# Four more hidden units by seven products, half loads of `y0`, first values in rows, a new written order

## The chip, the cores and the metric

The kernel runs on one core of one Trainium2 chip. The metric is the device time of one execution in microseconds (us), as the median of several runs of the same program; lower is better.

## The reference

Three computations follow each other on 2304 tokens (4 batches of 576): an attention whose softmaxes stand on q and k apart, a gated layer (called layer a here), and a second layer with Softplus (layer b). Cut to what is computed:

```python
def _attn_ref(q, k, v):            # (4, 8, 576, 64)
    q_s = softmax of q over the 64 features
    k_s = softmax of k over the 576 positions
    kv = np.einsum('bhsd,bhse->bhde', k_s, v)
    return np.einsum('bhsd,bhde->bhse', q_s, kv)

def _moe_ref(x, w_gate, w_val, w_out, rms_g):   # 512 -> 1536 -> 512
    xn = x / np.sqrt(np.mean(x * x, axis=-1, keepdims=True) + 1e-06) * rms_g
    g = xn @ w_gate
    return g * (1.0 / (1.0 + np.exp(-g))) * (xn @ w_val) @ w_out

def _moe2_ref(x, w_in, w_out):                  # 512 -> 2048 -> 512
    h = x @ w_in
    g = np.maximum(h, 0.0) + np.log1p(np.exp(-np.abs(h)))
    return g @ w_out
```

The attention's result, put back to 2304 rows of 512, goes through `_moe_ref` and then `_moe2_ref`. q and k are drawn with factors of 8 and 5.126.

## The kernel before

**Arithmetic.** Nearly every product is made of halves: a number is split into a high part and what is left of it, and `mm3` (L932 to L935) issues three matmuls, high by high (L933), high by low (L934) and low by high (L935). Large products go "by seven": a product of 2 x 2 blocks is made from seven block products of sums and differences of the blocks instead of eight, as in Strassen's method, and its sums run on the other engines.

**Tiling.** Tokens come in blocks of 384 (`T`); two blocks make a run. In layer b there are three runs, and each goes through the hidden dimension in eight units of 256 (`NPB` = 8): units 0 to 7 belong to the first run, 8 to 15 to the second, 16 to 23 to the third. Per unit: seven `H` steps (`h_mul`, L1271) make the hidden values; `HC` and `HD` copy and add them, `SP` (L1297) is Softplus on ScalarE; `SU` (`act_sum`) makes sums of them for products by seven; `BH` and `BL` (`act_h`, `act_l`, L1237 to L1247) make the high and low halves. Then the unit's part of the output: by four block products, as `Y` steps (`y_mul`, L1304: 512 columns per matmul, added up over the units in six PSUM banks, one for each of two token halves `o` and three chunks `t` of 128 tokens, and copied out by `YE`), or by seven, as `YP` steps (`y_part`, L1353: 21 per unit, 256 columns per matmul; products 1 to 4 are taken out of PSUM for each unit by `YC` or `YA`, the latter an addition on VectorE at L1380, products 5 to 7 add up in PSUM; `YX` joins the results of a run). Which units go by seven is the set `BY7` (L1262): before, units 8 to 21. The first run's eight units go by `Y`.

**Weights.** Weights arrive as 64-bit floats; `F` fetches a part, `CA` (Abs on ScalarE, L491), `CL` and `CD` (VectorE or GpSimd, L496 to L510) turn it into 32-bit floats. `TU` and `PS` make sums of blocks, `WH` (L587) and `WL` (L593) halves, `KO` (`keep_w`, L595) stores them into DRAM (`kept<-ws`), `WB` (`load_b`, L1266) loads them for each unit that uses them (`w<-kept`). The units of the first run thus read weights that were stored not long before: their names are `hx1`, `hx2`, `hx3`, `hx4` (first layer's blocks) and `y0`, `y1`, `yc`, `yd` (second layer's). `yc` and `yd` are the sums by seven: `VA`, `VS`, `VH`, `VL` (L1419 to L1448) make them for later runs and `VK` stores them.

**The order.** All is written out by hand: `ORDER` (L25 to L325) is a list of 4005 steps, executed by the loop at L1488. A step is a name and indices; a last letter says the engine (V VectorE, A ScalarE, P GpSimd). Each engine's queue is served in the order in which the list issues to it, and all DMAs stand in one queue, SP's. `HOMES` (L327 to L353) says which buffer each taking of a pooled tile uses: 16 tiles `w` (1024 columns, a ring for weights), 3 `ws` (work tiles of weights), 8 PSUM banks, 6 `hl`, 7 `h`, 3 `bits`, 2 each of `raw`, `s`, `a`, `ln`. A step that takes a tile waits until the tile's last reader, often a DMA, is done.

**The start.** `LV` (`load_v`, L632) and `LW` (L639) load a batch's values into `v_t`, whose rows have 64 values of two heads and a column of ones; batch 0 takes eight DMAs, one for each head, in pieces of 256 bytes, and two for the rest. `K3` (L759) multiplies the exponentials of k by them; the column of ones gives the denominators. `B` steps (`busy`, L977) issue matmuls of the identity that nobody reads.

The lines that the change touches are `load_v`, `load_vx`, `k3`, `act_h`, `BY7`, `load_b`, `h_softplus`, `y_mul`, `act_sum`, `y_part`, `y_join`, `w2_h`, and the two lists.

## Time and profile before

| | |
|---|---|
| median of 3 runs | 906.39 us (904.86 to 910.32) |
| the profiled execution | 907.15 us |
| its span in the profile | 905.4 us |
| TensorE (PE) busy | 880.7 us, 97% |
| VectorE (DVE) busy | 739.7 us, 82% |
| ScalarE (ACT) busy | 445.4 us, 49% |
| GpSimd (POOL) busy | 337.4 us, 37% |
| moved by DMA | 226.70 MB, mean 250 GB/s |

The profile is of one execution, times in us from the start of its span. Busy time is that in which an engine executes; a wait is idle time with the event that ended it. Matmuls overlap, so the duration of one is longer than the distance to the next one's start. "SPq" is SyncE issuing DMAs. The granted clock (PEclk) is the share of full speed that the chip gives TensorE.

### The profile page before, as it was taken

The page shows a single profiled execution, that of the slowest core. Times are in us where ns is not written, and L with a number is a line of the kernel's source. Part 1 is how long each engine was busy: PE and PEld are TensorE (multiplying, and loading weights), DVE is VectorE, ACT ScalarE, POOL GpSimd, SP SyncE. Part 2 cuts the span into 40 slices and gives each one's busy share as a digit, 9 for nine tenths or more (in the row PEclk, how much of TensorE's full clock was granted, in tenths as well). Part 3 has the DMA queues.
Part 4 walks back from the last instruction along what each step waited for, and adds up shares of the span by engine and source line. Part 5 has one row for each costly group of instructions (what it writes and reads, how often), then busy time and mean ns, then how long its engine had stood idle before and what let it go on. Part 6 is the DMA issues. An engine that isn't in the chain of part 4 may idle for free.

```text
span 905.4 us, 14902 instructions
## 1 busy us (share of the span) xinstructions
PE 880.7 (97%) x5296; PEld 848.6 (94%) x5296; DVE 739.7 (82%) x1365; ACT 445.4 (49%) x885; POOL 337.4 (37%) x302
## 2 busy tenths in 40 slices
PE   8899999999999999999999999989899999999998
PEld 8799999999999999999999998778799999999996
DVE  7999788697789998998989985767688676887764
ACT  3686665233566645555557756455343233342221
POOL 4543453233533223212342334423445347343312
PEclk9999999999999999999999999989999999999999
DMA  9995342342878898887999998876989887796942
GB/s 254 222 247 134 98 127 84 94 128 70 278 287 330 316 318 302 299 284 285 323 345 336 319 325 286 299 274 220 326 317 326 287 285 242 254 307 216 347 154 70
DMA packets 118011, 226.70 MB, mean 250 GB/s; under 512 B 31024, under 2 KB 72240, under 8 KB 117936
## 3 DMA queue, kind: packets, MB, share of 16 engines
q1 hardware_dynamic: 117936, 225.74, 73.8%
q8 instruction: 42, 0.69, 0.3%
q14 instruction: 33, 0.27, 0.1%
HBM read 169.87 MB, written 55.84 MB: 249 GB/s over the span
## 4 chain that ended last, share of the span: by engine, by line
PE 73%; DVE 11%; DMA 8%; ACT 3%; issue 2%; SPq 1%; POOL 1%; ACTq 0%; DVEq 0%; POOLq 0%
PE ps L933 23%; PE ps L934 23%; PE ps L935 23%; DMA kept<-ws 3%; PE ps L861 2%; DMA w<-kept 2%; DMA spilled<-bits 2%; PE ps L766 1%; DVE bits L506 1%; DVE bits L510 1%; DMA raw<-in_moe_w_out_dram 1%; PE ps L888 1%; SPq L635 1%; DVE h L1247 1%; DVE bits L502 1%
## 5 line engine op out<-in xcount | busy, mean ns | idle before, releaser
L933 PE MATMUL ps<-hl,w 128*128 128x384 f32 x284 | 99.3, 350 | 0.0
L934 PE MATMUL ps<-hl,w 128*128 128x384 f32 x284 | 95.2, 335 | 1.2 <-DVE hl L930 1.2
L935 PE MATMUL ps<-hl,w 128*128 128x384 f32 x284 | 95.1, 335 | 0.0
L933 PE MATMUL ps<-xy,w 128*128 128x384 f32 x218 | 74.4, 341 | 3.1 <-DMA w<-kept 2.3
L935 PE MATMUL ps<-w,h 128*128 128x256 f32 (+1 forms) x215 | 70.8, 329 | 3.3 <-DVE h L1247 3.3
L934 PE MATMUL ps<-xy,w 128*128 128x384 f32 x218 | 73.5, 337 | 0.0
L935 PE MATMUL ps<-xy,w 128*128 128x384 f32 x218 | 73.5, 337 | 0.0
L933 PE MATMUL ps<-w,h 128*128 128x256 f32 (+1 forms) x215 | 70.4, 328 | 1.6 <-DMA w<-kept 1.1
L934 PE MATMUL ps<-w,h 128*128 128x256 f32 (+1 forms) x215 | 70.3, 327 | 0.0
L1380 DVE TENSOR_TENSOR x<-ps,x 128x512 f32<-128x512 f32 x72 | 49.0, 687 | 25.8 <-PE ps L935 25.5
L933 PE MATMUL ps<-h,w 128*128 128x384 f32 x192 | 64.5, 336 | 0.9 <-ACT ps L1251 0.9
L935 PE MATMUL ps<-h,w 128*128 128x384 f32 x192 | 64.2, 334 | 0.0
L934 PE MATMUL ps<-h,w 128*128 128x384 f32 x192 | 64.2, 334 | 0.0
L934 PEld LDWEIGHTS ps<-hl,w 128*128 128x128 f32 x284 | 53.4, 188 | 2.4 <-DVE hl L930 1.5
L933 PEld LDWEIGHTS ps<-hl,w 128*128 128x128 f32 x284 | 53.4, 188 | 2.0 <-ACT s L1004 0.4
L491 ACT ACTIVATE bits<-raw 128x512 f32<-128x512 f32 x53 | 35.4, 672 | 39.0 <-DMA spilled<-bits 10.7
L935 PEld LDWEIGHTS ps<-hl,w 128*128 128x128 f32 x284 | 53.3, 188 | 0.0
L1247 POOL TENSOR_TENSOR h<-a,h 128x384 fp32r<-128x384 f32 x24 | 27.0, 1127 | 63.6 <-DVE h L1243 39.4
L935 PEld LDWEIGHTS ps<-w,h 128*128 128x128 f32 x215 | 41.0, 191 | 7.2 <-DVE h L1247 3.7
L933 PEld LDWEIGHTS ps<-xy,w 128*128 128x128 f32 x218 | 41.2, 189 | 6.7 <-DVE ws L593 2.6
L933 PEld LDWEIGHTS ps<-w,h 128*128 128x128 f32 x215 | 41.1, 191 | 5.8 <-DMA w<-kept 1.1
L506 DVE SCALAR_TENSOR_TENSOR bits<-raw,bits 128x512 int32<-128x512 int32 x62 | 46.0, 743 | 0.6
(488 smaller groups left out, 2914.7 us busy)
## 6 DMA issues: line engine op xcount, KB each, us to landing
w<-kept SPq DMA_DIRECT2D x93, 512.0 KB, 5.6
kept<-ws SPq DMA_DIRECT2D x56, 512.0 KB, 5.6
xy<-outside SPq DMA_DIRECT2D x22, 768.0 KB, 7.9
raw<-in_moe_w_out_dram SPq DMA_DIRECT2D x26, 512.0 KB, 5.3
hl<-outside SPq DMA_DIRECT2D x24, 384.0 KB, 7.1
raw<-in_moe_w_in_dram SPq DMA_DIRECT2D x16, 512.0 KB, 5.1
outside<-hl SPq DMA_DIRECT2D x18, 384.0 KB, 3.7
qe<-outside SPq DMA_DIRECT2D x8, 768.0 KB, 7.3
```

The source lines that it names most:

```text
L491: nc.scalar.activation(out=b.bitcast(F32), in_=hi, func=AF.Abs)
L502: nc.vector.tensor_scalar(out=b, in0=b, scalar1=3, scalar2=0x3FFFFFF8, op0=ALU.logical_shift_left, op1=ALU.bitwise_and)
L506: nc.vector.scalar_tensor_tensor(out=b, in0=words[:, :, 1], scalar=-0x40000000, in1=b, op0=ALU.bitwise_and, op1=ALU.bitwise_or)
L510: nc.vector.scalar_tensor_tensor(out=b, in0=words[:, :, 0], scalar=29, in1=b, op0=ALU.logical_shift_right, op1=ALU.bitwise_or)
L635: nc.sync.dma_start(out=v_t[:, m, :R, o * D:(o + 1) * D], in_=v[b, h, :SM].rearrange("(p r) d -> p r d", r=R))
L766: nc.tensor.matmul(out=ps[:, i, :], lhsT=ke_t[lo][:, i, r], rhs=v_t[:, m, r, :], start=(r == 0), stop=(r == R))
L861: nc.tensor.matmul(out=ps[:, s:s + n], lhsT=kvb[b % 2][:, m, :], rhs=qT_t[:, m, s:s + n], start=True, stop=True)
L933: nc.tensor.matmul(out=ps, lhsT=wh, rhs=xh, start=first, stop=False, skip_group_check=more)
L934: nc.tensor.matmul(out=ps, lhsT=wh, rhs=xl, start=False, stop=False, skip_group_check=more)
L935: nc.tensor.matmul(out=ps, lhsT=wl, rhs=xh, start=False, stop=last, skip_group_check=more)
L1247: engine[e].tensor_tensor(out=h[:, 1], in0=part[u, (f, o)], in1=h[:, 0].bitcast(F32), op=ALU.subtract)
L1380: nc.vector.tensor_tensor(out=tot, in0=ybank.pop((u, pair, t)), in1=tot, op=ALU.add)
```

## The change

Four things are done at once.

1. Units 4 to 7 of the first run go by seven (`TURN` = 4; `BY7` now begins at 4). Its six sums of units 0 to 3 end at unit 3 (`last` in `y_mul`); the new step `YT` (`y_turn`, 12 steps) turns them, by one copy and three subtractions for each chunk, into the totals to which products 1 to 4 of units 4 to 7 are added; `y_join` gets a way of its own for run 0, in the totals' own tiles. `yc` and `yd` of units 4 to 7 are now wanted in the first run: `w2_h` makes them in a tile of the ring `w` instead of `ws`. Some activations of units 4 to 6 take `hl` tiles instead of `raw` and `bits` (`act_h`, `spare`).
2. Units 8 to 21 load only the first 256 columns of `y0` (512 KB become 256 KB), the half that products by seven read.
3. Batch 0's values are loaded in rows as they stand in the input (`v_rows`, `v_rest`): four DMAs of two heads each in pieces of 1 KB, and one for the rest. `K3` of batch 0 has the ones in a matmul of its own, so that each of its matmuls becomes two. `MW` fills the end of the rest with zeros.
4. `ORDER` and `HOMES` are new throughout, from the first line.

Steps in the list, where their number changes (all steps: 4005 before, 4126 after):

| step | before | after | | step | before | after |
|---|---|---|---|---|---|---|
| Y | 122 | 74 | | BH, BL | 186 each | 198 each |
| YP | 294 | 378 | | SU | 56 | 72 |
| YA | 72 | 96 | | LV | 8 | 10 |
| YX | 28 | 42 | | MW | 0 | 1 |
| YE | 6 | 0 | | B (matmuls in them) | 6 (70) | 4 (48) |
| YT | 0 | 12 | | | | |

Each matmul of a `B` stands in the profile as two records. Takings of tiles in `HOMES`: `w` 220 before, 228 after; `ws` 94 and 80; `hl` 72 and 84; PSUM banks 454 and 481.

The lists in the diff are cut to their first lines; the rest is whole.

```diff
@@ -23,333 +23,343 @@
 ORDER = """
-LQ.0.0 LQ.0.1 Q0.0.0 QS.0.0.1.V MK LK.0.1.1 QS.0.0.0.P QE.0.0.1 LK.0.2.2 MX Q0.0.1 K0.0.1.1.1.V QS.0.1.1.V QE.0.0.0 QR.0.0
-LX.0 K0.0.1.1.2.V QS.0.1.0.P LQ.0.2 QI.0.0 QM.0.0.1.P K0.0.2.2.1.V QE.0.1.0 LK.0.0.1 F.5 QE.0.1.1 QR.0.1 CA.5.A QM.0.0.0.P
-B.0.31 T.0 QI.0.1 QM.0.1.0.P K0.0.1.1.3.V QM.0.1.1.P K0.0.0.1.1.R Q0.0.2 F.0 K0.0.2.2.2.V T.1 CA.0.A QS.0.2.0.V CL.5.V
...
+LQ.0.0 Q0.0.0 LQ.0.1 LK.0.1.1 QS.0.0.1.V LQ.0.2 Q0.0.1 K0.0.1.1.1.V QS.0.0.0.P QE.0.0.1 LK.0.2.2 QS.0.1.0.P QS.0.1.1.V
+QE.0.0.0 QR.0.0 LK.0.0.1 K0.0.1.1.2.V LX.0 MX QE.0.1.1 QI.0.0 QE.0.1.0 QR.0.1 K0.0.2.2.1.V K0.0.1.1.3.V K0.0.1.1.4.V MW
+K0.0.2.2.2.V F.3 QI.0.1 Q0.0.2 QM.0.0.1.P MK F.0 K0.0.0.1.1.R QM.0.0.0.P CA.0.A B.0.40 K1.0.0 KM.0.0 F.5 K0.0.2.2.3.V B.1.3
...
@@ -605,7 +615,11 @@
 
 
     k_t = kv_p.tile([P, H, R + 1, D], F32, name="k_t")
-    v_t = kv_p.tile([P, KD, R + 1, 2 * D + 1], F32, name="v_t")
+    v_all = kv_p.tile([P, KD * (R + 1) * (2 * D + 1)], F32, name="v_t")
+    v_t = v_all.rearrange("p (m r c) -> p m r c", m=KD, r=R + 1)
+    v_rows = v_all[:, :H * R * D].rearrange("p (h r d) -> p h r d", h=H, r=R)
+    v_rest = v_all[:, H * R * D:H * (R + 1) * D].rearrange("p (h d) -> p h d", h=H)
+    ROWS = 1
     km_t = kv_p.tile([P, H, D], F32, name="km_t")
 
 
@@ -630,6 +644,11 @@
         nc.sync.dma_start(out=k_t[:SX, :, R], in_=k[b, :, SM:].rearrange("h p d -> p h d"))
 
     def load_v(b, h0=0, h1=H):
+        if b < ROWS:
+            nc.sync.dma_start(
+                out=v_rows[:, h0:h1], in_=v[b, h0:h1, :SM].rearrange("h (p r) d -> p h r d", r=R)
+            )
+            return
         for h in range(h0, h1):
             m, o = divmod(h, 2)
             nc.sync.dma_start(
@@ -637,6 +656,9 @@
             )
 
     def load_vx(b):
+        if b < ROWS:
+            nc.sync.dma_start(out=v_rest[:SX], in_=v[b, :, SM:].rearrange("h p d -> p h d"))
+            return
         for o in range(2):
             nc.sync.dma_start(
                 out=v_t[:SX, :, R, o * D:(o + 1) * D], in_=v[b, o::2, SM:].rearrange("m p d -> p m d")
@@ -763,6 +785,13 @@
         for i in range(n):
             m = lo + i
             for r in range(R + 1):
+                if b < ROWS:
+                    hs = slice(2 * m, 2 * m + 2)
+                    rhs = v_rows[:, hs, r] if r < R else v_rest[:, hs]
+                    out_ = ps[:, i, :2 * D].rearrange("p (o d) -> p o d", o=2)
+                    nc.tensor.matmul(out=out_, lhsT=ke_t[lo][:, i, r], rhs=rhs, start=(i == 0 and r == 0), stop=True, skip_group_check=True)
+                    nc.tensor.matmul(out=ps[:, i, 2 * D:], lhsT=ke_t[lo][:, i, r], rhs=ones, start=False, stop=True, skip_group_check=True)
+                    continue
                 nc.tensor.matmul(
                     out=ps[:, i, :], lhsT=ke_t[lo][:, i, r], rhs=v_t[:, m, r, :], start=(r == 0), stop=(r == R)
                 )
@@ -1034,6 +1063,9 @@
             nc.gpsimd.memset(v_t[:, :, :, 2 * D:], 1.0)
             nc.gpsimd.memset(v_t[SX:, :, R, :2 * D], 0.0)
 
+        def v_zeros(_=None):
+            nc.gpsimd.memset(v_rest[SX:], 0.0)
+
         def kv_zeros(_=None):
             for t in kvb:
                 nc.gpsimd.memset(t, 0.0)
@@ -1041,6 +1073,7 @@
         eng2 = {"V": "dve", "P": "pool", "A": "act"}
         ops = {
             "MV": v_ones,
+            "MW": v_zeros,
             "MK": kv_zeros,
             "MX": load_kx_least,
             "LX": load_kx,
@@ -1236,7 +1269,10 @@
 
         def act_h(u, f, o, e):
             if (f, o) in ((2, 1), (2, 3)):
-                h = take(raw_p, "raw", [P, 2 * 512], F32R)[:, :2 * T].rearrange("p (h t) -> p h t", h=2)
+                if u - NU < NPB - 1:
+                    h = take(hl_p, "hl", [P, 2, T], F32R)
+                else:
+                    h = take(raw_p, "raw", [P, 2 * 512], F32R)[:, :2 * T].rearrange("p (h t) -> p h t", h=2)
             else:
                 h = act_tile()
             hbs[u, f, o] = h
@@ -1259,14 +1295,15 @@
         def o_end(u, o, m, e):
             copy[e](out=x2t[2 * RUNS[RUN_OF[u]][1] + o][:, m], in_=acc.pop((u, o, m)))
 
-        BY7 = set(range(NPB, 2 * NPB)) | set(range(2 * NPB, 3 * NPB - 2))
+        TURN = 4
+        BY7 = set(range(TURN, 2 * NPB)) | set(range(2 * NPB, 3 * NPB - 2))
 
         wb = {}
 
         def load_b(u, name):
-            n = 256 if name == "hx4" else 512
+            n = 256 if name == "hx4" or (name == "y0" and u >= NPB and u in BY7) else 512
             w = wb[name, u] = ring()
-            nc.sync.dma_start(out=w[:, :, :n].bitcast(F32), in_=kept[name, u % NPB])
+            nc.sync.dma_start(out=w[:, :, :n].bitcast(F32), in_=kept[name, u % NPB][:, :, :n])
 
         def h_mul(u, k):
             r = len(RUNS) - 3 + u // NPB
@@ -1287,9 +1324,14 @@
             t = part[u + NU, PLACE[k]] = part.pop((u, SUM_OF[k], "h"))
             nc.vector.tensor_tensor(out=t, in0=bk[u, "h", SEVEN[k][3]], in1=t, op=ALU.add)
 
+        def spare(u):
+            if u < NPB - 1:
+                return take(hl_p, "hl", [P, 2, T])[:, 0]
+            return bits_tile(None).bitcast(F32)[:, :T]
+
         def h_softplus(u, f, o):
             if (f, o) == (1, 0):
-                t = bits_tile(None).bitcast(F32)[:, :T] if u in BY7 else take(fa, "a", [P, T])
+                t = spare(u) if u in BY7 else take(fa, "a", [P, T])
                 part[u + NU, (f, o)] = t
                 src = bk[u, "h", 0]
             else:
@@ -1311,7 +1353,7 @@
             c = slice(t * P, (t + 1) * P)
             n = side(half)
             more = half is not None
-            last = p == NPB - 1 or (p == NPB - 2 and (i, o, t) == (2, 0, NCB - 1))
+            last = p == (NPB if i else TURN) - 1 or (p == NPB - 2 and (i, o, t) == (2, 0, NCB - 1))
             mm3(acc[jp, o, t][:, n], h[:, 0, c], h[:, 1, c], w[:, 0, n], w[:, 1, n], first, last and f != o, more)
 
         def y_end(jp, o, t, *how):
@@ -1340,7 +1382,7 @@
                 2: ((0, 0), (2, 1), (0, 0), ALU.subtract),
                 4: ((1, 0), (1, 0), (2, 2), ALU.subtract),
             }[i]
-            t = part[u, (2, i)] = part[u, out] if out else bits_tile(None).bitcast(F32)[:, :T]
+            t = part[u, (2, i)] = part[u, out] if out else spare(u - NU)
             engine[e].tensor_tensor(out=t, in0=part[u, x], in1=part[u, y], op=op)
 
         Y7 = {
@@ -1352,7 +1394,9 @@
 
         def y_part(u, k, t):
             i = u // NPB
-            if k < 5:
+            if k < 5 and i == 0:
+                key, half = (u, k in (1, 4), t), k in (1, 3)
+            elif k < 5:
                 key, half = (u, (k - 1) // 2, t), (k - 1) % 2
             elif t < 2:
                 key, half = (i, k), t
@@ -1363,7 +1407,7 @@
                 ybank[key] = bank()
             ps = ybank[key][:, 256 * half:256 * half + 256]
             at, wn, side_ = Y7[k]
-            h, w, n = hbs[(u + NU, *at)], wb[wn, u], side(side_)
+            h, w, n = hbs[(u + NU, *at)], wb[wn, u] if (wn, u) in wb else w2[wn, u], side(side_)
             c = slice(t * P, (t + 1) * P)
             mm3(ps, h[:, 0, c], h[:, 1, c], w[:, 0, n], w[:, 1, n], first, k < 5, True)
 
@@ -1378,6 +1422,21 @@
         def y_add(u, pair, t):
             tot = y_total(u // NPB, pair)[:, t]
             nc.vector.tensor_tensor(out=tot, in0=ybank.pop((u, pair, t)), in1=tot, op=ALU.add)
+
+        def y_turn(t, n, e):
+
+            a, b = acc[2, 0, t], acc[2, 1, t]
+            x, y = (y_total(0, pair)[:, t] for pair in range(2))
+            base = y[:, side(1)]
+            if n == 0:
+                copy[e](out=base, in_=b[:, side(1)])
+                return
+            out, p, q, op = (
+                (x[:, side(0)], a[:, side(0)], base, ALU.subtract),
+                (x[:, side(1)], a[:, side(1)], base, ALU.subtract),
+                (y[:, side(0)], base, b[:, side(0)], ALU.subtract),
+            )[n - 1]
+            nc.vector.tensor_tensor(out=out, in0=p, in1=q, op=op)
 
         yres = {}
 
@@ -1399,6 +1458,22 @@
                     ys[jp, o, t] = yres[jp, o][:, t]
                 return yres[jp, o][:, ts, side(half)]
 
+            if i == 0:
+                t2, t3, t4, t1 = (y_total(0, pair)[:, ts, side(h)] for pair in range(2) for h in range(2))
+                out, x, y, op = (
+                    lambda: (t2, t1, t2, ALU.add),
+                    lambda: (t3, tot(5), t3, ALU.add),
+                    lambda: (t1, tot(6), t1, ALU.add),
+                    lambda: (t3, t1, t3, ALU.add),
+                    lambda: (t1, tot(7), t1, ALU.add),
+                    lambda: (t4, t1, t4, ALU.subtract),
+                    lambda: (t1, tot(5), t1, ALU.add),
+                )[n]()
+                for o in range(2):
+                    for t in range(NCB)[ts]:
+                        ys[jp, o, t] = y_total(0, o)[:, t]
+                engine[e].tensor_tensor(out=out, in0=x, in1=y, op=op)
+                return
             out, x, y, op = (
                 lambda: (res(0, 0), tot(1), tot(2), ALU.add),
                 lambda: (tot(1), tot(6), tot(1), ALU.add),
@@ -1435,7 +1510,7 @@
             engine[e].tensor_tensor(out=out, in0=x, in1=y, op=ALU.subtract)
 
         def w2_h(p, f, e):
-            w = wt["y" + "cd"[f], p] = work()
+            w = wt["y" + "cd"[f], p] = w2["y" + "cd"[f], p] = work() if p < TURN else ring()
             copy[e](out=w[:, 0], in_=w2[p, f])
 
         def w2_l(p, f, e):
@@ -1453,6 +1528,7 @@
             "YC": y_copy,
             "YA": y_add,
             "YX": y_join,
+            "YT": y_turn,
             "YS": y_sum,
             "VA": w2_whole,
             "VS": w2_sum,
```

## Rows read from the trace of the kernel before

**Rows 1.** The page: span, busy times, granted clock of TensorE in 40 slices

```profile
span 905.4 us, 14902 instructions
...
PE 880.7 (97%) x5296; PEld 848.6 (94%) x5296; DVE 739.7 (82%) x1365; ACT 445.4 (49%) x885; POOL 337.4 (37%) x302
...
PEclk9999999999999999999999999989999999999999
```

**Rows 2.** Windows: length; PE, PEld, DVE, ACT, POOL busy (instructions); clock; DMA; GB/s

```profile
200.00:300.00 100.00, 100.00 (x579) 100.00 (x578) 84.26 (x148) 53.14 (x113) 36.49 (x31) 1.00 0.65 238
300.00:500.00 200.00, 198.85 (x1132) 195.45 (x1131) 183.43 (x355) 115.54 (x253) 56.84 (x49) 1.00 0.88 313
```

**Rows 3.** Short windows, TensorE alone: length, busy (matmuls), clock, DMA share, GB/s

```profile
591.00:595.00 4.00, 0.84 (x4) 0.94 0.66 245
595.00:601.00 6.00, 5.84 (x15) 0.50 0.57 201
601.00:607.00 6.00, 6.00 (x30) 0.97 0.93 305
637.00:639.00 2.00, 0.00 (x0) 0.97 0.98 324
639.00:643.00 4.00, 3.38 (x9) 0.59 1.00 339
```

**Rows 4.** Timelines of ScalarE, then VectorE: start, length, what, [idle before, releaser]

```profile
587.37 0.62 ACT L587 CAST ws<-bits 128x512 fp32r<-128x512 f32 x1 [4.42 <-DMA kept<-ws]
...
592.23 1.28 ACT L491 ACT_TABLE_LOAD   x1
593.52 0.66 ACT L491 ACTIVATE bits<-raw 128x512 f32<-128x512 f32 x1
...
594.21 0.43 DVE L496 TENSOR_SCALAR bits<-bits 128x512 f32<-128x512 f32 x1 [3.38 <-ACT bits L491]
594.55 0.55 DVE L1247 TENSOR_TENSOR h<-a,h 128x384 fp32r<-128x384 f32 x1
```

**Rows 5.** The chain that ended last, 626 to 644 us: start, length, what

```profile
626.98 7.80 DMA kept<-ws
...
635.42 7.71 DMA w<-kept
...
643.17 0.50 PE ps L933
```

**Rows 6.** Timeline of TensorE in two places: matmuls of 512 and 256 columns

```profile
626.68 0.39 PE L933 MATMUL ps<-w,h 128*128 128x512 f32 x1
...
631.48 0.33 PE L933 MATMUL ps<-xy,w 128*128 128x384 f32 x1
...
803.44 0.28 PE L933 MATMUL ps<-w,h 128*128 128x256 f32 x1
...
804.87 0.34 PE L933 MATMUL ps<-xy,w 128*128 128x384 f32 x1
```

**Rows 7.** The page's groups: count, busy us, mean ns of one, idle before, releaser

```profile
L1380 DVE TENSOR_TENSOR x<-ps,x 128x512 f32<-128x512 f32 x72 | 49.0, 687 | 25.8 <-PE ps L935 25.5
```

**Rows 8.** Windows of the second layer, columns as in rows 2

```profile
510.00:660.00 150.00, 142.17 (x698) 127.47 (x697) 110.40 (x191) 79.48 (x145) 54.33 (x49) 0.97 0.83 292
660.00:860.00 200.00, 199.46 (x1377) 196.90 (x1377) 153.18 (x271) 71.47 (x148) 91.84 (x83) 1.00 0.82 284
```

**Rows 9.** Timeline of the start: SyncE issuing the values, `K3` on TensorE

```profile
15.64 8.37 SPq L635 DMA_DIRECT2D v_t<-in_v_dram  x8
...
24.48 2.47 PE L766 MATMUL ps<-v_t,xy 128*128 128x129 f32 x20 [0.31 <-issue]
```

**Rows 10.** A window of the start, columns as in rows 2

```profile
15.00:20.00 5.00, 3.81 (x35) 3.62 (x34) 5.00 (x13) 1.53 (x3) 0.81 (x3) 1.00 1.03 287
```

**Rows 11.** DMA issues: count, KB each, median us from issue to landing

```profile
v_t<-in_v_dram SPq DMA_DIRECT2D x32, 128.0 KB, 4.5
k_t<-in_k_dram SPq DMA_DIRECT2D x2, 256.0 KB, 5.7
```

More of the change, by code (lines that the diff above doesn't have):

```diff
@@ new lines @@
+BH.11.0.0.A H.0.2 KO.56.1 VH.0.1.V WB.2.hx1 BL.11.0.0.V OC.10.0.3.A WB.1.hx1 SI.11.6 U.11.6 HD.0.1 ZL.9.t1.V SI.11.5
+VH.0.0.A WB.3.hx3 OP.10.1.2.A ZS.9.t4.V OM.10.1.3 BH.11.1.0.A H.0.3 BH.11.1.1.A WB.1.y0 SP.0.0.0 BL.11.1.0.V HC.0.2.A
+OP.11.0.3.A VL.0.0.V HC.0.3.V VL.0.1.P OC.10.1.1.A WB.2.y0 OC.10.1.3.A VA.1.1.V CL.57.V BH.12.0.0.A OM.10.1.2 VA.1.0.V
+CD.57.0 CD.57.1 H.0.4 VK.0.1 OP.11.0.0.A H.0.5 F.58 H.1.1 VS.1.1.V HD.0.4 HD.0.5 ZH.9.t4.qe0.A WH.54.1.A BL.11.1.1.V
+OC.10.1.2.A ZL.9.t4.V WB.1.hx4 OM.10.1.0 SP.0.0.1 VS.1.3.V OC.10.1.0.A SP.0.1.1 WL.54.1.P OM.11.0.0 H.1.0 H.0.6 CA.58.A
@@ new lines @@
+s 010110010110100101001010010101010110101101001001010110010101110101100101001010101010101010
+a 010110011001100010101010010010100101010011001010110101101101101110011010110101010101010100
+h 01101001100101234563524065234163052314635024613205423612054163201456203561423506104213650241546310256240125341
+h 62501363142631032415203164205130652435106251064230526103261302145036125046132540
+ws 01201211020120012102102101021201212102102120102101201202120120120120102010200102
+ln 010101010101010101010101101010101010101010
```

627 lines of the change are left out of this document (313 added, 314 removed).

## The prediction, made before the result was known

> **What bounds the kernel now.** I read the page's busy times first: TensorE is busy 880.7 of 905.4 us, and its granted clock is below full in one slice of forty [rows 1]. So the time is TensorE's list of matmuls, plus the few places where it waits or runs slow. Two long windows come next [rows 2]: from 200 to 300 us TensorE issues 579 matmuls with VectorE 84% busy; from 300 to 500, with the same 384-column matmuls throughout, it issues 1132 where twice 579 would be 1158, while VectorE is 92% busy. A crowded VectorE thus costs TensorE 26 / 1158 = 2.2%. The short windows show where most of the rest goes [rows 3]. From 601 to 607 us 30 matmuls go in 6 us, 0.2 us each. From 591 to 595 only 4 go, so 16 are missing, 3.2 us; from 595 to 601, at a granted clock of 0.50, 15 go, so 15 are missing, 3.0 us. The second place is 637 to 639, without a matmul (2.0 us), and 639 to 643 at a clock of 0.59 with 9 instead of 20 (2.1 us). Together 6.2 + 4.1 = 10.3 us, half of it not waiting but the half clock after it.
>
> What ended those waits, on the engines' timelines: ScalarE stood 4.42 us for a store out of a `ws` tile to land; then, as at each Abs (L491) that stands between Softplus activations (L1297), it loaded a table first; VectorE, whose queue is in order, stood 3.38 us until Abs had run, and the low half that TensorE wanted (L1247) came at 594.55 [rows 4]. For the second wait the chain is plain: a store of 7.80 us, the load of the same weights released by it, 7.71 us, then the matmul [rows 5]. So both long stalls are transfers that landed late, one freeing a `ws` tile, one making unit 7's weights pass through DRAM.
>
> **The change, part by part.** The sum is made against the profiled execution's 907.15 us; the median of the three runs is 0.76 lower, and I take that off at the end.
>
> *Four more units by seven.* 48 `Y` steps go, each three 512-column matmuls; 84 `YP` steps come, each three of 256. In the timeline 21 of 512 columns start between 626.68 and 631.48, 0.2286 us each; 12 of 256 between 803.44 and 804.87, 0.119 each [rows 6]. So 48 x 3 x 0.2286 = 32.9 goes, 84 x 3 x 0.119 = 30.0 comes: **-2.9 us**, certain as long as TensorE is the bound; a 256-column matmul gives back 4% of its gain.
>
> What this costs the others: 24 `YA` of 0.687 on VectorE [rows 7], 16 `SU`, 12 `YT`, 14 `YX` for 6 `YE`, 12 more `BH` and `BL`. Counted in the two orders between `H.0` and `H.8`, steps lettered V rise from 116 to 147, A from 91 to 142. At 0.6 us a step, between the 0.55 of L1247 [rows 4] and the 0.687 of L1380 [rows 7], that is 18.6 us for VectorE, which is busy 110.4 of the 150 us there [rows 8]: 129 of about 150, 86%, with part of the `YA` behind it. It is nearer to the 92% of 300 to 500 us than to the 84% of 200 to 300, so I take the loss of 2.2% over the 180 us from 510 to 690: **+3.9 us**. Bounds: 0, if it behaves as at 84%, and 8, twice the loss.
>
> *Late landings.* Three edits bear on the stalls. `VH` of units 4 to 7 takes 8 tiles from `w` instead of `ws`, and six `YE` tiles go: 80 takings of the three `ws` tiles instead of 94, which lightens the wait of [rows 4]. Counted in the orders, loads with under 7 us of TensorE work between the freeing of their slot and their first use fall from 8 to 3. Against it, unit 7 still passes through DRAM: from `KO` to first use the order leaves 6.0 us of matmuls for `hx4` (4.2 before) but 6.7 for `hx3` (9.4 before), where the chain needed 7.80 + 7.71 [rows 5]; what helps is that stores are issued well ahead of their place in the list. I take both stalls as gone, **-10.3 us**. Bounds: 0, if both return, and -13, if TensorE's other idle time from 510 to 860 us goes too: it idles 7.8 + 0.5 us there [rows 8], of which 3.2 + 0.2 + 2.0 + 0.6 lie in the windows of [rows 3], so some 2.3 are left.
>
> *Table loads.* Abs on ScalarE stands between Softplus steps six times now, nine times after, two loads each: six more loads of 1.29 us from the load to the next activation [rows 4], 7.7 us. ScalarE is busy 79.5 of 150 us there [rows 8]; with 51 steps of 0.5 and these it is at 112 us: hidden on the whole, and if not, a load holds its queue as in the first stall. Cost 0, upper bound in the rivals. The Trainium skill's page "ScalarE: Activation LUTs", section "What ACT_TABLE_LOAD costs", says that a switch costs 2.66 us, 1283 ns of load and a drain; by it the six would be 16 us. The rows agree on the load and show no drain.
>
> *First values in rows, and the start.* Batch 0's values come in four transfers with 1 KB pieces instead of eight with 256 B: the sync queue spent 8.37 us on the eight, so some 4 us of issuing go. `K3` of batch 0 gets 40 more matmul records of 0.12 us (20 in 2.47), +4.9; the filler `B` falls from 140 records to 96, at the same price -5.4 [rows 9]. All of it stands beside a VectorE that is busy 5.00 of 5 us in that stretch, where TensorE is busy 3.81 [rows 10], so I take 0. Without that cover the start could lose 5 us (the added `K3`) or win 4 (the issuing), of which I take 3.
>
> *Half loads of `y0`.* 14 loads of 512 KB become 256 KB. They belong to the units after the eighth, where TensorE is busy 199.46 of 200 us [rows 8]: nobody waits, 0; at best the 0.5 us that is missing there.
>
> Sum: 907.15 - 2.9 - 10.3 + 3.9 = 897.85; less 0.76: **897.1 us**.
>
> **Rivals.** *The stalls stay.* The round trip of unit 7 is no roomier for `hx3`, and three more Abs stand among the Softplus steps; the pieces of [rows 4, 5] are all still in the program. Then only the matmuls count: 907.15 - 2.9 + 3.9 - 0.76 = 907.4 with both stalls, 901.2 with one. Against it: more room at the loads, fewer takings of `ws`.
>
> *VectorE becomes the bound, slower than before.* From `H.0` to `H.8` the matmuls need 132 us; VectorE needs 129 and reached at most 92% in any window of [rows 2], so the stretch would take 140: 8 us of waiting. If it comes in waits as long as those of [rows 3], the half clock doubles it to 16. With the two stalls (DMA, not VectorE) still there: 906.4 - 2.9 + 16 = 919.5. It decides from a lag of about 12 us. For it: 31 more steps in order on one queue. Against it: where VectorE was at 92% no clock fell.
>
> *The start and the small waits go too.* The order is new from the first line. With -13 for the waits, no crowding and -3 at the start: 906.4 - 2.9 - 13 - 3 = 887.5, up to 893. For it: TensorE idles 1.2 of the 5 us from 15 to 20 us [rows 10]. Against it: VectorE is full there and the work up to the first output steps is the same. The Trainium skill's page "DMA: Bandwidth & Descriptors", section "Specifications", gives 512 B as the least size for line rate; by it the values land sooner and this case gains. The rows lean that way: 128 KB of values in 256 B pieces land in 4.5 us, 256 KB of keys in 1 KB pieces in 5.7 [rows 11].
>
> **How the numbers follow.** About 1% (9 us) is what a measurement of this kernel tells from no change: 897.3 and 915.5 are the borders. Forecast 0.40, 893 to 902, half of it on each side of 897.3. The stalls stay 0.24, 901 to 908: same 0.22, slower 0.02 when a third joins. VectorE bound 0.12, 908 to 920: same 0.05, slower 0.07. Start and small waits too 0.24, 886 to 894: faster. So faster 0.44, same 0.47, slower 0.09. The range 888 to 910 leaves out the lower quarter of the last case, 0.07, and most of VectorE's, 0.11; the forecast's own range is 893 to 902.
>
> **What would show it.** The matmul records fall by 144 and rise by 252 (+40 -44 at the start), to about 5400, and TensorE's busy time falls by some 3 us apart from stalls. Right on the stalls: no window after 500 us with a granted clock under 0.9, and no wait of TensorE over 1 us on a load or on L1247. Right on the crowding: VectorE 85 to 92% from 500 to 690 us, with many waits under 0.5 us. Wrong would be a half clock in that stretch (the stalls came back; see whether a store's landing stands before it), VectorE at 95% with waits of TensorE on L1247 or on the sums, or the first 60 us more than 3 us longer or shorter.

## The result

The changed kernel took 899.82 us (median of 11 runs, 895.62 to 902.77) where the kernel before took 905.61 us (11 runs); the ratio is 0.9919, with a 95% interval of 0.9897 to 0.9941. The profiled execution took 900.87 us. So the time fell by 0.8%, within the 1% that was called no change, and within the forecast's own range. What follows shows that two terms behind the number, one stall's going (-6.2 us) and the crowding (+3.9 us), were wrong and in part cancelled, and that some 6 us came from a stretch that the sum did not have: that the number held is in good part luck.

The page of the changed kernel, its first line, busy times and granted clock in 40 slices (they answer to [rows 1]):

```profile
span 898.8 us, 15177 instructions
...
PE 877.9 (98%) x5400; PEld 856.2 (95%) x5400; DVE 737.6 (82%) x1396; ACT 475.2 (53%) x941; POOL 335.6 (37%) x304
...
PEclk9999999999999999999999999999999999999999
```

TensorE has 104 records more (108 = 252 - 144 from the products by seven, 40 from `K3`, 44 less from `B`), and is busy 2.8 us less. ScalarE is busy 30 us more. Four windows, columns as in [rows 2], and the waits of TensorE between 510 and 690 us (us in total, times, longest):

```profile
300.00:450.00 150.00, 150.00 (x866) 149.78 (x865) 138.85 (x266) 91.43 (x203) 40.85 (x37) 1.00 0.90 321
450.00:510.00 60.00, 57.20 (x321) 56.88 (x320) 53.37 (x101) 36.40 (x77) 11.67 (x9) 0.97 0.91 314
510.00:600.00 90.00, 84.55 (x430) 77.39 (x429) 73.69 (x141) 69.23 (x123) 20.41 (x17) 0.98 0.86 299
600.00:690.00 90.00, 88.90 (x601) 87.10 (x600) 83.44 (x153) 53.08 (x104) 46.16 (x41) 1.00 0.89 312
```

```profile
PE ps L962 <- ACT ln L1321: 2.5, 1, 2.5
PE ps L962 <- ACT x L1296: 1.1, 1, 1.1
PE ps L962 <- DVE x L1424: 0.7, 1, 0.7
PE ps L962 <- DVE s L1325: 0.7, 1, 0.7
PE ps L962 <- ACT s L1321: 0.6, 1, 0.6
PE ps L962 <- ACT a L1321: 0.6, 1, 0.6
PE ps L962 <- DVE x L1439: 0.4, 1, 0.4
```

No wait on a load is left in that stretch; four of the seven are on ScalarE, the other three, 1.8 us, on VectorE, of which `YA` (L1424) and `YT` (L1439) are steps that the change added. The longest, on ScalarE's timeline (the VectorE step that it held, and the matmul after it, stand behind):

```profile
578.81 1.28 ACT L1339 ACT_TABLE_LOAD   x1
580.11 0.53 ACT L1339 ACTIVATE a<-a 128x384 f32<-128x384 f32 x1
...
581.07 1.28 ACT L501 ACT_TABLE_LOAD   x1
582.36 0.66 ACT L501 ACTIVATE bits<-raw 128x512 f32<-128x512 f32 x1
...
583.32 0.48 ACT L1321 COPY ln<-ps 128x384 f32<-128x384 f32 x1
...
583.05 0.43 DVE L506 TENSOR_SCALAR bits<-bits 128x512 f32<-128x512 f32 x1 [2.33 <-ACT bits L501]
...
583.85 0.69 PE L962 MATMUL ps<-xy,w 128*128 128x384 f32 x1 [2.53 <-ACT ln L1321]
```

The copy that empties the PSUM bank TensorE wants (L1321 at 583.32) stands in ScalarE's queue behind two table loads, an Abs, two Softplus activations and a cast; VectorE's clamp waits for the same Abs. And a stall that the kernel before did not have: on the chain that ended last, a load of w_in, and on the timelines VectorE's first instruction after it and the matmul that it held:

```profile
464.39 8.45 DMA raw<-in_moe_w_in_dram
```

```profile
472.93 0.69 DVE L497 SCALAR_TENSOR_TENSOR bits<-raw 128x512 f32<-128x512 f32 x1 [3.12 <-DMA raw<-in_moe_w_in_dram]
...
476.27 0.45 PE L963 MATMUL ps<-h,w 128*128 128x384 f32 x1 [2.80 <-DVE h L1283]
```

**Where the time went.** To compare whole executions I worked out, from the starts of all matmuls in the timeline, the *list* (each matmul at the usual distance to the next start of its form: 0.1735 us for 384 columns, 0.230 for 512, 0.120 for 256, 0.112 for most of those of 128 columns or fewer) and the *loss* (what the distances are longer than that: waits and half clock). List plus loss is the time from the first matmul to the last. In us, by stretch of the span:

| kernel | list | 0-100 | 100-300 | 300-450 | 450-510 | 510-600 | 600-690 | from 690 | loss |
|---|---|---|---|---|---|---|---|---|---|
| before | 862.5 | 11.1 | 4.3 | 3.0 | 1.6 | 9.5 | 6.1 | 1.2 | 36.8 |
| changed | 859.1 | 15.6 | 1.2 | 0.1 | 4.6 | 8.6 | 2.7 | 1.1 | 34.0 |
| a_again | 859.1 | 13.9 | 1.1 | 0.0 | 2.6 | 9.0 | 3.0 | 1.0 | 30.8 |
| a_copy | 859.1 | 15.0 | 1.2 | 0.5 | 4.9 | 1.4 | 3.0 | 1.1 | 27.1 |
| b_copy | 862.5 | 11.1 | 3.5 | 3.2 | 1.6 | 2.6 | 1.9 | 1.2 | 25.2 |
| a_fill | 862.7 | 10.0 | 1.2 | 0.0 | 5.3 | 6.9 | 2.6 | 1.0 | 27.1 |
| a_abs_v | 859.1 | 15.5 | 1.1 | 0.1 | 4.6 | 2.6 | 2.9 | 1.1 | 27.9 |
| b_abs_v | 862.5 | 13.6 | 2.9 | 3.7 | 2.9 | 3.5 | 4.1 | 0.9 | 31.5 |
| a_53 | 859.1 | 15.7 | 1.1 | 0.1 | 1.1 | 7.9 | 3.8 | 1.0 | 30.7 |
| a_best | 859.1 | 13.5 | 1.2 | 0.0 | 1.6 | 3.1 | 5.1 | 1.5 | 26.0 |
| b_round | 862.5 | 11.2 | 4.2 | 2.8 | 3.1 | 8.5 | 1.0 | 0.4 | 31.1 |
| a_rows0 | 854.7 | 18.2 | 1.1 | 0.1 | 1.5 | 7.3 | 4.3 | 1.1 | 33.6 |
| a_y0full | 859.1 | 13.1 | 1.2 | 0.0 | 4.6 | 8.4 | 4.1 | 1.1 | 32.5 |

One profile of a kernel lies up to 3.6 us from its median, so a row is read for its stretches and the medians and ratios for the total. The change gives 3.4 us of list, 6 us between 100 and 450 us, about 4 us between 510 and 690 us, and pays 3 to 4.5 us at the start and 1 to 3 us at 450 to 510 us.

### The profile page after: what moved, and what is told of

It is laid out like the page before. It is cut to its first block, busy times and chain, and to the rows that moved or that the text cites. A ratio compares the mean times of both kernels' runs of the same rounds, so it can differ in the third digit from the quotient of the medians.

```text
span 898.8 us, 15177 instructions
## 1 busy us (share of the span) xinstructions
PE 877.9 (98%) x5400; PEld 856.2 (95%) x5400; DVE 737.6 (82%) x1396; ACT 475.2 (53%) x941; POOL 335.6 (37%) x304
## 4 chain that ended last, share of the span: by engine, by line
PE 79%; DVE 12%; ACT 3%; issue 2%; DMA 2%; POOL 0%; DVEq 0%; POOLq 0%; ACTq 0%
PE ps L962 25%; PE ps L963 25%; PE ps L964 25%; PE ps L890 2%; DMA raw<-in_moe_w_in_dram 1%; DVE xy L730 1%; DMA raw<-in_moe_w_out_dram 1%; PE ps L917 1%; DVE km_t L697 1%; DVE bits L516 1%; DVE bits L512 1%; DVE qm L819 1%; DVE h L1283 1%; DVE qs L841 1%; ACT L501 1%
## 5 line engine op out<-in xcount | busy, mean ns | idle before, releaser
L962 PE MATMUL ps<-hl,w 128*128 128x384 f32 x280 | 98.4, 351 | 0.0
L963 PE MATMUL ps<-hl,w 128*128 128x384 f32 x280 | 93.9, 335 | 0.0
L964 PE MATMUL ps<-hl,w 128*128 128x384 f32 x280 | 93.8, 335 | 0.0
L1424 DVE TENSOR_TENSOR x<-ps,x 128x512 f32<-128x512 f32 x96 | 64.7, 685 | 29.2 <-PE ps L964 28.6
L962 PE MATMUL ps<-xy,w 128*128 128x384 f32 x236 | 80.4, 341 | 3.1 <-ACT ln L1321 2.5
L963 PE MATMUL ps<-xy,w 128*128 128x384 f32 x236 | 79.9, 338 | 0.0
L964 PE MATMUL ps<-xy,w 128*128 128x384 f32 x236 | 79.8, 338 | 0.0
L962 PE MATMUL ps<-w,h 128*128 128x256 f32 (+1 forms) x203 | 62.9, 310 | 2.3 <-ACT x L1296 1.1
L964 PE MATMUL ps<-w,h 128*128 128x256 f32 (+1 forms) x203 | 62.5, 308 | 0.0
L963 PE MATMUL ps<-w,h 128*128 128x256 f32 (+1 forms) x203 | 62.3, 307 | 0.0
L962 PEld LDWEIGHTS ps<-hl,w 128*128 128x128 f32 x280 | 52.8, 188 | 1.3 <-issue 0.3
L963 PEld LDWEIGHTS ps<-hl,w 128*128 128x128 f32 x280 | 52.8, 189 | 1.0 <-issue 0.3
L964 PEld LDWEIGHTS ps<-hl,w 128*128 128x128 f32 x280 | 52.7, 188 | 0.0
L962 PEld LDWEIGHTS ps<-xy,w 128*128 128x128 f32 x236 | 44.9, 190 | 4.1 <-ACT ln L1321 2.8
L1296 ACT COPY x<-ps 128x384 f32<-128x384 f32 x72 | 33.9, 483 | 23.7 <-PE ps L964 23.3
L516 DVE SCALAR_TENSOR_TENSOR bits<-raw,bits 128x512 int32<-128x512 int32 x62 | 45.0, 727 | 0.7
L963 PEld LDWEIGHTS ps<-xy,w 128*128 128x128 f32 x236 | 45.0, 191 | 0.1
L964 PEld LDWEIGHTS ps<-xy,w 128*128 128x128 f32 x236 | 44.9, 190 | 0.0
L520 DVE SCALAR_TENSOR_TENSOR bits<-raw,bits 128x512 int32<-128x512 int32 x62 | 44.3, 715 | 0.7
```

The source lines that it names most:

```text
L516: nc.vector.scalar_tensor_tensor(out=b, in0=words[:, :, 1], scalar=-0x40000000, in1=b, op0=ALU.bitwise_and, op1=ALU.bitwise_or)
L520: nc.vector.scalar_tensor_tensor(out=b, in0=words[:, :, 0], scalar=29, in1=b, op0=ALU.logical_shift_right, op1=ALU.bitwise_or)
L962: nc.tensor.matmul(out=ps, lhsT=wh, rhs=xh, start=first, stop=False, skip_group_check=more)
L963: nc.tensor.matmul(out=ps, lhsT=wh, rhs=xl, start=False, stop=False, skip_group_check=more)
L964: nc.tensor.matmul(out=ps, lhsT=wl, rhs=xh, start=False, stop=last, skip_group_check=more)
L1296: copy[e](out=x2t[2 * RUNS[RUN_OF[u]][1] + o][:, m], in_=acc.pop((u, o, m)))
```

## The experiments

Their names begin with a for an edit of the changed kernel and with b for one of the kernel before. Ratios are to the kernel before, run beside them.

**The changed kernel again (a_again).** No edit.

> The changed kernel once more, untouched. The profiled execution of it showed two new stalls: TensorE waits 3.0 us at 473 us behind a load of w_in that took 8.45 us to land, and 2.7 us at 581 us while ScalarE loads its tables twice, each followed by some 6 us at the half clock. If both belong to the written order, this profile shows both again at the same places, within a few us, and the time is 899 +/- 3 us (0.99 of before). If the first is chance (a transfer that happened to land late), it is gone here and the time is 3 to 5 us shorter, about 895.

Measured: 898.13 us, ratio 0.9915 (0.9888 to 0.9942). Both stalls are there, at 471 us (2.0 us) and 577 us (2.7 us); in the later kernels with the same order around them they come again, the first between 1.4 us (a_rows0) and 3.6 us (a_fill), the second at 2.7 us each time. They belong to the order; the length of the first varies. The loss in the first 100 us differs by 1.7 us between the two profiles.

**Copies for the absolute values, in both kernels (a_copy, b_copy).** The same edit, from part 58 in the changed kernel and from part 60 in the one before; it leaves out the absolute value and with it the table loads:

```diff
-            nc.scalar.activation(out=b.bitcast(F32), in_=hi, func=AF.Abs)
+            if n >= 58:
+                nc.scalar.copy(out=b.bitcast(F32), in_=hi)
+            else:
+                nc.scalar.activation(out=b.bitcast(F32), in_=hi, func=AF.Abs)
```

> The changed kernel, in which ScalarE copies the high words of the ten weight parts from 58 on instead of taking their absolute value (the weights of these parts come out wrong; the instruction's size is the same). Copy needs no table, so the table loads between the Softplus steps are gone, some 18 loads of 1.28 us. Theory (the loads stand on the path at 581 us): the 2.7 us stall there and the half clock behind it are gone, 4 to 5 us less than the changed kernel, about 895. Rival (the loads are hidden by ScalarE's idle time, as the prediction took them): the same time as the changed kernel within 1 us, the stall is still there with VectorE or a transfer as its releaser.

> The kernel before, in which ScalarE copies the high words of the parts from 60 on instead of taking their absolute value (their weights come out wrong). The table loads between Softplus steps are gone, twelve of 1.28 us. If the stall at 591 us was the table loads' (two of them stand between 588.4 and 593.5 us), it is gone with the half clock behind it: 5 to 6 us less than before, about 900. If it was the store out of the work tile that landed late, as the prediction read it (ScalarE stood 4.42 us for it first), the stall stays at about its length less the 2.6 us of two loads: 906 less 0 to 3.

Measured: 890.80 us, ratio 0.9832 (0.9801 to 0.9863), and 898.09 us, ratio 0.9914 (0.9887 to 0.9940). The table loads cost 7.3 us in the changed kernel and 7.5 us in the one before, and nearly all of it leaves the loss from 510 us on: from 9.0 to 1.4 us between 510 and 600 us in the one, from 15.6 to 4.5 us between 510 and 690 us in the other. My reading of the stall at 591 us falls with it. ScalarE's timeline of b_copy in the same place:

```profile
586.25 0.62 ACT L590 CAST ws<-bits 128x512 fp32r<-128x512 f32 x1 [6.25 <-DMA kept<-ws]
586.77 0.51 ACT L1246 CAST h<-s 128x384 fp32r<-128x384 f32 x1
587.19 0.65 ACT L492 COPY bits<-raw 128x512 f32<-128x512 f32 x1
587.75 0.52 ACT L1300 ACTIVATE a<-a 128x384 f32<-128x384 f32 x1
588.27 0.66 ACT L492 COPY bits<-raw 128x512 f32<-128x512 f32 x1
```

and the waits of its TensorE from 510 to 690 us:

```profile
PE ps L936 <- DMA w<-kept: 0.8, 1, 0.8
PE ps L936 <- ACT x L1263: 0.6, 1, 0.6
PE ps L936 <- ACT a L1300: 0.4, 1, 0.4
```

ScalarE waits for a store out of a `ws` tile as before, even longer (6.25 us where [rows 4] has 4.42), and no matmul stands over 0.8 us: the late store alone stops nobody. In the kernel before three table loads stand between the store's landing at 587.37 us and the Abs that VectorE waited for; [rows 4] show the last of them, and these are the others:

```profile
588.42 1.28 ACT L491 ACT_TABLE_LOAD   x1
...
590.39 1.28 ACT L1297 ACT_TABLE_LOAD   x1
```

From the cast after the store to the end of the second Abs ScalarE takes 6.8 us there, and 2.7 us to the end of the second copy in b_copy. So the stall needs the loads; whether they would have made it without the late store was not tried. Without table loads both kernels lose the same between 510 and 690 us, 4.4 and 4.5 us, though VectorE is busy 163.9 us of those 180 in a_copy and 141.6 in b_copy:

```profile
510.00:600.00 90.00, 89.76 (x469) 82.77 (x468) 81.22 (x154) 55.28 (x119) 25.33 (x22) 1.00 0.89 316
600.00:690.00 90.00, 88.59 (x612) 87.31 (x612) 82.70 (x150) 47.49 (x98) 46.34 (x41) 1.00 0.89 314
```

(These are the windows of a_copy.) So in sum the added steps of VectorE cost TensorE nothing that these profiles show. They are not free of waits, though: the one wait of a_copy's TensorE in that stretch is on `YA` (L1424, three lines further down here), and b_copy has none on VectorE.

```profile
PE ps L965 <- DVE x L1427: 1.4, 1, 1.4
```

**The absolute values on VectorE (a_abs_v, b_abs_v).** The letter of ten steps in the changed kernel and of six in the one before:

```diff
-... CA.58.A ... CA.59.A ... (to CA.67.A)
+... CA.58.V ... CA.59.V ... (to CA.67.V)
```

> The changed kernel with the absolute values of parts 58 to 67 on VectorE instead of ScalarE: the same results, no table load between the Softplus steps, and ten more instructions of 0.68 us on VectorE between 510 and 690 us. With copies instead (no table, no more work for VectorE) the kernel took 890.8 us where the changed kernel took 898.1, and TensorE lost 1.4 instead of 9.0 us between 510 and 600 us. If only the loads matter, this takes 891 +/- 2 us. If a crowded VectorE costs TensorE (the prediction's 2.2% in a stretch of 180 us, or VectorE as the bound), the 6.8 us of VectorE come back in part: 894 to 898 us.

> The kernel before with the six absolute values that stand on ScalarE among the Softplus steps (parts 60, 61, 63, 64, 65, 67) on VectorE, all else as it was. With copies in their place the kernel took 898.1 us against 905.6. If the table loads made the stalls at 591 and 637 us, this gets nearly all of it: a ratio of 0.991 to 0.993, and both stalls are under 1 us. The ratio of the changed kernel with the same repair to this one then says what the change is worth without the table loads: 0.993 if they cost the same in both kernels, 0.987 if the change pays more without them.

Measured: 894.24 us, ratio 0.9844 (0.9820 to 0.9868), and 898.32 us, ratio 0.9929 (0.9905 to 0.9954). This keeps most of what the copies gave. In us the first lies at the edge of the second case, but the kernel before took 908.05 us beside it, 2.5 us more than beside the copies; by the ratio it is the first case. The 10 steps more of VectorE go with 1.2 us more of loss between 510 and 600 us (2.6 against 1.4, one profile each). I had expected both stalls to be short in b_abs_v; they are not: a wait at 636 us for a load out of `kept` is still 2.2 us. The three pairs of ratios give what the change is worth in each setting:

| absolute values | before | changed | changed to before |
|---|---|---|---|
| on ScalarE | 1 | 0.9919, 0.9915 | 0.992 |
| copies on ScalarE | 0.9914 | 0.9832 | 0.992 |
| on VectorE | 0.9929 | 0.9844 | 0.991 |

Each is uncertain by some 0.003 to 0.004. The change is worth 0.8% with the table loads and without them. So the six loads that it adds cost nothing that the medians show (7.3 us for 18 loads, 7.5 for 12), and it gains as much where both stalls are short beforehand.

**Part 53 behind the low halves (a_53).**

```diff
-... F.53 U.9.4 D.10.1.v WL.51.1.V CA.53.V OM.9.0.0 CL.53.V F.55 CD.53.0 C.10.3.g.A KO.47.3 BH.9.1.1.A WL.52.1.V M.10.3.v CD.53.1 ZI.8.t4.hl BL.9.0.1.V BL.9.1.1.V M.10.5.g ...
+... F.53 U.9.4 D.10.1.v WL.51.1.V OM.9.0.0 F.55 C.10.3.g.A KO.47.3 BH.9.1.1.A WL.52.1.V M.10.3.v ZI.8.t4.hl BL.9.0.1.V BL.9.1.1.V CA.53.V CL.53.V CD.53.0 CD.53.1 M.10.5.g ...
```

> The changed kernel with four steps of VectorE (the conversion of weight part 53) moved behind seven others in the list, among them three low halves that TensorE waits for. In four profiles of this order TensorE stands 2.0 to 3.6 us at 471 to 473 us, with VectorE standing at the first of the four until a load of w_in has landed 8.45 us after its issue. Theory (a late landing stops a whole queue in order; what stands behind it is what TensorE lacks): the stall goes, TensorE's lost time from 450 to 510 us falls from 2.6 to 5.3 us to about 1, the time is 2 to 4 us less than the changed kernel, 894 to 896. Rival (part 53 itself is late, and its halves are next on the path): the stall moves behind and the time stays at 898 +/- 1.

Measured: 895.84 us, ratio 0.9873 (0.9850 to 0.9896), about 4 us under the changed kernel's. VectorE still waits for the load, but behind the halves:

```profile
470.34 0.55 DVE L1283 TENSOR_TENSOR h<-ln,h 128x384 fp32r<-128x384 f32 x1
470.81 0.55 DVE L1283 TENSOR_TENSOR h<-a,h 128x384 fp32r<-128x384 f32 x1
472.50 0.69 DVE L497 SCALAR_TENSOR_TENSOR bits<-raw 128x512 f32<-128x512 f32 x1 [1.14 <-DMA raw<-in_moe_w_in_dram]
```

The loss between 450 and 510 us falls to 1.1 us. Moving what waits for the load was enough. Why it was late the chain of the changed kernel shows: it was issued at 464.39 us, when VectorE's own step at 463.76 us (L520, 0.61 us) had freed its tile, and took 8.45 us to land, where the 16 loads of w_in have a median of 5.0.

**Both repairs (a_best), and the longer filler with them (a_best_fill).**

> The changed kernel with both repairs: the absolute values of parts 58 to 67 on VectorE, and the conversion of part 53 behind the three low halves. Alone the first gave a ratio of 0.984 and the second 0.987, where the changed kernel has 0.992. If the two stalls are separate losses the ratios add up: 0.980 +/- 0.002, about 889 us by a before of 907, with under 1.5 us lost from 450 to 510 us and under 3 us from 510 to 600 us. If a stall removed only moves its loss to the next late thing, 0.983 to 0.985.

> The same with 56 instead of 40 matmuls of the identity in the first filler. In the changed kernel the longer filler brought the clock of the start back to 1.00 and the time stayed within its scatter (0.9907 against 0.9915). Expected: the same as the one without within 1 us, as the work done by 100 us was the same with either. If the clock of the start does count, 1 to 2 us less.

Measured: 890.20 us, ratio 0.9842 (0.9817 to 0.9868), and 892.91 us, ratio 0.9856 (0.9833 to 0.9880). By the ratios the two do not add up, which would be 0.980: a_best is no faster than a_abs_v, within the intervals. Nor is it by the table: from 100 us on it loses 12.5 us, a_abs_v 12.4. The loss at 450 to 510 us is gone (1.6 against 4.6), and 2.2 us of it come back between 600 and 690 us (5.1 against 2.9). The longer filler gave nothing (0.9856). The waits of a_best's TensorE there, and its window of 510 to 600 us:

```profile
PE ps L962 <- DVE x L1424: 1.7, 1, 1.7
PE ps L962 <- DVE s L1325: 1.2, 1, 1.2
PE ps L962 <- DVE x L1439: 0.4, 1, 0.4
```

```profile
510.00:600.00 90.00, 88.36 (x460) 80.74 (x459) 85.00 (x160) 47.57 (x105) 25.82 (x22) 1.00 0.87 310
```

The additions of the products by seven (L1424, `YA`) and the sums of `HD` (L1325) now come late. VectorE is busy 85.0 of 90 us just before; but it is busy 84.6 in a_abs_v, whose longest wait on it is 0.4 us. So VectorE is the next to be waited for, as in a_copy, and its busy share does not tell when; why it lags here was not tried. Both are 1.4 to 1.6% under the kernel before and some 0.7% under the changed one.

**The load without its store (b_round).**

```diff
-in_=kept[name, u % NPB])
+in_=kept[name, 6 if u == 7 and name in ("hx3", "hx4") else u % NPB])
```

> The kernel before, in which unit 7 loads the first-layer weights hx3 and hx4 of unit 6 instead of its own (so these products of unit 7 are wrong), which were stored long before: the load does not wait for a store. If the stall at 637 us is the round trip through DRAM, as the prediction read the chain, it goes with its half clock, 4 us less than before, about 901 to 902. If the table loads make it (without them it shrank to 0.6 us), the store was only late because the weights were made late, and the stall then is at most moved to the next thing that is made late: 904 to 906. The stall at 591 us stays in either case.

Measured: 902.82 us, ratio 0.9953 (0.9931 to 0.9974), 4 us. Waits of its TensorE from 510 to 690 us:

```profile
PE ps L935 <- DVE h L1247: 3.3, 1, 3.3
PE ps L933 <- ACT a L1297: 0.7, 2, 0.5
PE ps L933 <- ACT s L1284: 0.7, 1, 0.7
PE ps L933 <- DMA w<-kept: 0.2, 1, 0.2
```

The stall at 637 us is gone with its half clock (the loss from 600 to 690 us falls from 6.1 to 1.0 us), the one at 591 us is untouched. So the round trip is needed for this stall, as the prediction said, but two things are to be added. First, the load of 7.71 us in [rows 5] is not the one that the stall waited for. That one, of `hx4`, was issued with the store's landing at 634.80 us and landed 4.28 us later; the load of 7.71 us is the next in the queue (`y1` of unit 6) and ended a later, short wait. TensorE's timeline in the kernel before:

```profile
639.22 0.66 PE L933 MATMUL ps<-xy,w 128*128 128x384 f32 x1 [2.31 <-DMA w<-kept]
...
643.17 0.50 PE L933 MATMUL ps<-w,h 128*128 128x512 f32 x1 [0.57 <-DMA w<-kept]
```

Second, the table loads are needed for it too: without them the round trip is still in the program and its store takes as long (7.52 us in b_copy, issued 10.4 us earlier, while TensorE is 7.5 us ahead there by the table), but the wait for `hx4` is gone in b_copy and 0.7 us in b_abs_v (whose 2.2 us are for `y1` of unit 6). Taking either away is enough. In the changed kernel the same store is issued at 626.77 us and the load behind it at 630.64, 3.9 us later where it was 7.8:

```profile
626.77 0.57 SPq L608 DMA_DIRECT2D kept<-ws  x1
...
630.64 0.53 SPq L1306 DMA_DIRECT2D w<-kept  x1
```

**The first filler longer (a_fill).**

```diff
-... CA.0.A B.0.40 K1.0.0 ...
+... CA.0.A B.0.56 K1.0.0 ...
```

> The changed kernel with 56 instead of 40 matmuls of the identity in the first filler, so that TensorE does not stand idle from 13.1 to 16.9 us. In the changed kernel's profile the granted clock was 0.70 from 15 to 20 us and 0.66 in two later stretches (40 to 45, 60 to 65 us); in the kernel before, with 70 such matmuls instead of 48, it was 1.00 throughout. Theory (the shorter filler costs the clock, and the clock the start): clock 1.00 from 15 to 25 us and 1 to 2 us less in all. Rival (the start is VectorE's, TensorE's clock does not matter there): the clock comes back and the time stays within 1 us. If the two later stretches at the half clock stay, they have causes of their own.

Measured: 897.23 us, ratio 0.9907 (0.9879 to 0.9935), the changed kernel's within the scatter. The window of 15 to 25 us, in a_again and then in a_fill:

```profile
15.00:25.00 10.00, 7.37 (x44) 7.13 (x45) 8.61 (x17) 4.38 (x7) 3.09 (x3) 0.67 0.95 267
```

```profile
15.00:25.00 10.00, 8.12 (x69) 7.59 (x68) 9.44 (x19) 5.03 (x8) 3.43 (x4) 1.00 0.98 297
```

The clock comes back from 0.67 to 1.00 and the time does not: by 100 us TensorE has done 70.0 us of its list other than filler and the matmuls added to `K3`, against 69.8 in a_again. So TensorE's clock does not set the start. Its longest wait in the first 50 us is on one step of VectorE (`km_t`), 3.8 us in the changed kernel and 4.9 in a_again, where the kernel before has 1.2; the longer filler shortens it to 1.3 and moves nothing.

**Values head by head (a_rows0).**

```diff
-    ROWS = 1
+    ROWS = 0
```

(and `MV` in the place of `MW` in the list).

> The changed kernel with batch 0's values loaded head by head in pieces of 256 bytes as before (eight transfers instead of four, two for the rest instead of one) and multiplied with the column of ones in the same matmul, all else in the new order. Prediction's step (the start belongs to VectorE, the transfers and the matmuls stand beside it): the same as the changed kernel within 1 us. If the values land late and are waited for: 2 to 5 us more. If the added matmuls (40 records, 4.6 us) stand on the path: 1 to 4 us less.

Measured: 897.79 us, ratio 0.9893 (0.9870 to 0.9916), no slower than the changed kernel. Its TensorE has 4.4 us less of list to do, and waits longer in the first 50 us, for the exponentials and for `kvb` (us in total, times, longest):

```profile
PE ps L890 <- DVE kvb L806: 2.7, 1, 2.7
PE ps L795 <- ACT xy L777: 2.6, 2, 2.1
```

Neither wait is on the values: loading them in rows gains nothing that can be seen here. The ratio lies some 2 us under the changed kernel's, inside the intervals, so it does not rule out that the added matmuls cost 1 to 4 us, the rival that I had named. The profile speaks against it: by 100 us TensorE has done the same list, other than filler and those matmuls, as in a_again (within 0.3 us), and this profile loses 1.1 to 3.1 us less at 450 to 510 us, which this edit does not touch.

**Whole loads of `y0` (a_y0full).**

```diff
-            n = 256 if name == "hx4" or (name == "y0" and u >= NPB and u in BY7) else 512
+            n = 256 if name == "hx4" else 512
```

> The changed kernel with whole loads of y0 for units 8 to 21 (512 KB instead of 256 KB), all else as it is. The prediction's step: nobody waits for them, 0, at most 0.5 us; the ratio stays at 0.992 and TensorE loses no more than 1 us from 690 us on, as with half loads. If the half loads are part of the gain (they make room for the stores and loads of 600 to 690 us), that stretch loses 1 to 4 us more and the ratio is 0.993 to 0.996.

Measured: 899.54 us, ratio 0.9925 (0.9897 to 0.9952): the same. Nobody waits for these loads.

## Why the prediction was right, and where it was not

The number held: 899.82 us in a range of 888 to 910, the forecast's case, and 2.7 us above its value. By its steps:

- **By seven, -2.9 us: right.** The list is 3.4 us shorter; 2.9 of it are the matmuls of 512 and 256 columns (144 x 0.230 - 252 x 0.120), the rest is the start's. This is counted from the records; no run took the products by seven away alone.
- **The stall at 637 us, -4.1 us: right in the outcome, half right in mechanism.** b_round shows that the round trip is needed; in the changed kernel its store takes half as long, no matmul waits for a load there, and the loss from 600 to 690 us is 3.1 to 3.4 us less. But the table loads are needed for the stall too (b_copy), and the 7.71 us of [rows 5], taken as the second half of its chain, belong to another load.
- **The stall at 591 us, -6.2 us: wrong.** The step that failed is the reading of [rows 4]: I took the store that landed late as what made the stall, saw one of the three table loads behind it, and took the loads as hidden by ScalarE's idle time ("Cost 0"). b_copy has the store's wait at 6.25 us and no stall. The loads that were there already, 7.5 us by the medians for both stalls together, were the price, and the changed kernel still pays 7.3: the loss from 510 to 600 us stayed at 8.6 to 9.0 us after 9.5. For the six loads that the change adds the 0 came out all the same, as the difference of these two, but by luck: an engine that is busy 79.5 of 150 us [rows 8] does not hide a load when what TensorE wants next stands behind it in its queue. The Trainium skill's page "ScalarE: Activation LUTs", section "What ACT_TABLE_LOAD costs", puts a price on each switch, which I cited and then set to nothing; its 1283 ns for the load agree with the rows, and what the runs gave back, 7.3 us for some 18 loads, is 0.4 us a load on average.
- **Crowding, +3.9 us: wrong in the rate.** The rule of 2.2% came from comparing two stretches of one kernel [rows 2]. In the changed kernel VectorE is busy 138.85 of 150 us from 300 to 450 us, 93%, where it was 137.05, and TensorE issues 866 matmuls where it issued 849; the loss is 0.1 us instead of 3.0. So it was not VectorE's busy share that slowed the kernel before there; of the four edits only the last, the order, touches that stretch. With 22 us more of VectorE between 510 and 690 us, a_copy loses what b_copy loses. What VectorE's added work does cost shows as single waits: 1.8 us on VectorE in the changed kernel there, 0.2 us in the kernel before but for the stall at 591 us.
- **What I did not have:** 6 us less loss between 100 and 450 us, from the new order, and 1 to 3 us more at 450 to 510 us, a head of a queue that waits for a load of 8.45 us (a_53: 4 us). That the start could go either way within 5 us was held: it loses 3 to 4.5 us more by 100 us, and by 200 us TensorE has done 167.2 us of useful list (without filler and the added matmuls of `K3`) where it had done 167.7; the a_again profile has 168.9. So 0 was right for it, and for the half loads and the rows.

Against the sum: -10.3 + 3.9 = -6.4 was to come from stalls and crowding; -2.8 and -6.0 came (the loss of the two profiles against 36.8), by other ways. *VectorE as the bound* did not happen in the changed kernel; the waits of 1.4 us in a_copy and 1.7 us in a_best show where it begins. *The stalls stay* was half true: one stayed, under the cause that I had called hidden. By the signs named beforehand, the half clock (0.80 from 585 to 590 us) said that a stall was back, and no store's landing stands before it; VectorE is busy 157.1 of 180 us from 510 to 690 us, 87%, inside the 85 to 92% that was to go with crowding.

Open: which moves in the new order made the 6 us between 100 and 450 us. The lists differ throughout, and no part of that was tried alone; nor were the four edits, but for the half loads and the rows; so what the 0.8% is made of is counted and read from profiles, not shown by a run. Of the 3.0 us that the kernel before loses between 300 and 450 us, the waits of the profile name only 0.4. Whether the copies' profiles, which lie 1.8 us apart where the medians lie 7.3, hide a stretch that varies between executions is open as well.
